# A DeltaNet and Fourier-mixing kernel on one core: two rounds of triangular inverses in turn, and the weights' conversion moved behind the first Fourier stage

## The chip, the cores and the metric

The kernel runs on one core of one Trainium2 chip. The metric is device microseconds (us) of one execution, smaller is better. Before the change the median of three runs is 840.67 us (838.32 to 844.29); the profiled execution took 837.88 us, of which the profile shows a span of 836.1 us.

The engines are TensorE (PE; its weight loads are shown as PEld), VectorE (DVE), ScalarE (ACT), GpSimd (POOL) and SyncE (SP), whose queue issues nearly all transfers here. Each engine works through its own instructions in order; semaphores order the engines among each other.

## The reference, cut to what matters

```python
# q, k, v: (4, 8, 768, 48) float32; beta: (4, 8, 768); w_ch1: (384, 1536), w_ch2: (1536, 384)
def _attn_ref(q, k, v, beta):                      # DeltaNet, token by token
    k_n = k / (norm(k) + 1e-06)
    for t in range(S):
        y[:, :, t] = q[:, :, t] @ state
        v_old = k_n[:, :, t] @ state
        state = state + beta[:, :, t] * outer(k_n[:, :, t], v[:, :, t] - v_old)
    return y

def _moe_ref(x, w_ch1, w_ch2):                     # x: y as (4, 768, 384)
    mixed = real(fft(fft(x, axis=1), axis=2))      # Fourier mixing
    u = x + mixed
    un = (u - mean(u)) / sqrt(var(u) + 1e-06)      # per row
    return u + maximum(un @ w_ch1, 0.0) @ w_ch2    # two-layer network
```

The two weight matrices reach the kernel as 64-bit floats. The kernel reads them as pairs of 32-bit integers and builds 32-bit floats from them with integer and float operations ("conversion").

## The kernel before

The tokens are worked on in groups of 128 (two chunks of 64), six groups to a batch of 768, 24 in all. Four groups make a round: the 32-by-32 triangular blocks of a round are inverted together, all 128 partitions side by side. The inverse is a loop of 31 steps, each of two VectorE operations, and every operation needs the result of the one ahead of it:

```python
def invert(r):                       # one round = 4 groups
    A = wk.tile([128, W, W], F32, tag="A", bufs=2); M = wk.tile([128, W, W], F32, tag="M")
    nc.gpsimd.memset(M, 0.0)
    nc.vector.transpose(A, G...)     # L291
    yield
    ...                              # norms of the keys: some 12 small VectorE operations, L298-314
    yield
    for j in range(W - 1):           # W = 32
        n = W - 1 - j
        t = wk.tile([128, 256], F32, tag="tmp")
        nc.vector.tensor_tensor(t, A[:, j+1:W, j:j+1]..., M[:, j:j+1, 0:j+1]..., op=ALU.mult)   # L320
        nc.vector.tensor_tensor(M[:, j+1:W, 0:j+1], M[:, j+1:W, 0:j+1], t, op=ALU.add)         # L323
        yield
    nc.vector.transpose(A..., M); nc.vector.transpose(G..., M...)                              # L326, L327
```

Around it stand, for each group g:

```python
def pre_a(g):   # keys: 4 transposes on PE -> KT (ACT L260), then 32 products K K^T (pair<-KT)
                # -> G (blocks to invert, ACT L279) and GX (the other blocks, ACT L281)
def pre_b(g):   # queries: 4 transposes -> QT (ACT); yield
                # K Q^T (pair<-QT,KT), masked into LQ (DVE L352); yield
                # mixing with the inverse: V scaled and MT built on GpSimd (L359, L363), two sets of
                #   32x32 products (one<-G,GX and one<-A,XM, evicted by ACT); yield; yield
                # W and U0 from MT, K and V (pair<-MT,K and one<-V,MT; ACT L403, L405)
def step(g, c): # the serial part, per chunk: S x W (PE) -> U (DVE L423) -> K x U (PE) -> S (DVE L442);
                # after the second chunk the output x: S x Q and U x LQ (PE), ACT L463, DVE L472
```

`fourier(b)` folds x into even and odd halves (GpSimd L489, L490; DVE L493 to L500), multiplies with two tables on PE (`pf`, `pb`) and adds the result to x with the statistics for the normalization (DVE L538 to L546). `mlp(b)` works on two tiles of 128 tokens at a time: transposes, 12 column blocks of the hidden layer (`ph`, evicted into `hT` by ACT L578 and DVE L580 in turn), then the second layer (`po`). 

The weights come in six pieces of 1536 elements per partition:

```python
def weights():
    n1, n2 = 1, DFF // DM            # w1 by blocks of 128 rows, w2 by four of them: 3 + 3 pieces
    ...
    w64s = [staged(0), staged(1)]    # staged: a tile of tag "big" (two buffers) and its transfer, L209
    yield
    for i, (_, dst) in enumerate(pieces):
        w64 = w64s[i]
        if 0 < i < len(pieces) - 1: w64s.append(staged(i + 1))
        lo, hi = w64[:, :, 0], w64[:, :, 1]
        man = wk.tile([128, DFF], F32, tag="F"); num = wk.tile([128, DFF], I32, tag="O")
        nc.scalar.activation(man, lo, Copy, ...)                      # L222
        nc.vector.tensor_scalar(num, hi, 0xFFFFF, ...)                # L223
        nc.vector.scalar_tensor_tensor(man, num, 2.0**-20, man, ...)  # L225
        yield
        num = wk.tile([128, DFF], I32, tag="O")
        nc.vector.tensor_scalar(num, hi, 20, 0x7FF, ...)              # L229
        nc.scalar.activation(num, num, Relu, bias=low_e)              # L231
        yield
        nc.vector.tensor_scalar(num, num, 255, 2.0**23, ...)          # L233
        nc.vector.scalar_tensor_tensor(num, hi, -2**31, num, ...)     # L235
        nc.gpsimd.tensor_tensor(dst, man, num, op=ALU.mult)           # L237
        yield
```

Tag "big" also holds the folded halves E of `fourier` and the hidden layer `hT` of `mlp`; tag "O" also holds O of `fourier`.

The driver: four `pre_a`, the queries of group 0, the inverse of round 0 alone, the rest of group 0; then twelve steps of batch 0, beside each of which run the preparation of the next group, the keys and the inverse of the next round, and half of the conversion. This part is in an order fixed by hand; from there on a list scheduler orders the program when it is built.

```python
with tc.manual_schedule(engines=engines):
    for g in range(RL): drain(pre_a(g)) ...
    pb = pre_b(0); drain(part(pb, 2)); drain(invert(0)); drain(pb)
    for n in range(2 * NL): one(n)          # steps of batch 0 and what goes beside them
for b in range(B):
    f = fourier(b)
    if b == 0: drain(f); drain(side)        # rest of the conversion
    else: run([(f, 1), (side, 1)])
    side, done = mlp(b), 0
    if b + 1 < B:
        for n in range(2*NL*(b+1), 2*NL*(b+2)): one(n)   # steps of batch b+1, with mlp(b) beside them
drain(side)
```

Of the kernel before, what the change touches and what calls it, by code (L numbers as in the profile page):

```python
# [58 lines left out]
def kernel(  # L59
# [84 lines left out]
    def load(g):  # L144
        if g < NLT:
            nc.sync.dma_start(out=Qs[g % 2][:, :, 0:D], in_=rows(q, g))
            halves(Ks[g % 3].rearrange("p (c j) d -> p c j d", c=2)[:, :, :, 0:D], k, g)
            Vs[g] = wk.tile([128, 2, 4, D], F32, tag="V", bufs=2, name="V")
            halves(Vs[g], v, g)
# [42 lines left out]
    def weights():  # L192

        if moe_w_ch1.dtype == F32:
            nc.sync.dma_start(out=w1, in_=moe_w_ch1.rearrange("(c p) f -> p c f", p=128))
            nc.sync.dma_start(out=w2, in_=moe_w_ch2.rearrange("(c p) m -> p c m", p=128))
            return
        w1v = moe_w_ch1.bitcast(I32).rearrange("(c p) (f two) -> p c f two", p=128, two=2)  # L200
        w2v = moe_w_ch2.bitcast(I32).rearrange("(c p) (m two) -> p c m two", p=128, two=2)
        n1, n2 = 1, DFF // DM
        pieces = [(w1v[:, i:i + n1], w1[:, i:i + n1]) for i in range(0, KD, n1)]
        pieces += [(w2v[:, i:i + n2], w2[:, i:i + n2]) for i in range(0, KF, n2)]

        def staged(i):
            t = wk.tile([128, DFF, 2], I32, tag="big", bufs=2, name="w64")
            src = pieces[i][0]
            nc.sync.dma_start(out=t.rearrange("p (c f) two -> p c f two", c=src.shape[1]), in_=src)  # L209
            return t  # L210

        w64s = [staged(0), staged(1)]
        yield
        for i, (_, dst) in enumerate(pieces):
            w64 = w64s[i]
            if 0 < i < len(pieces) - 1:
                w64s.append(staged(i + 1))
            lo, hi = w64[:, :, 0], w64[:, :, 1]
            man = wk.tile([128, DFF], F32, tag="F", name="man")
            num = wk.tile([128, DFF], I32, tag="O", name="num")  # L220

            nc.scalar.activation(man, lo.bitcast(U32), ACT.Copy, scale=2.0 ** -52, bias=1.0)  # L222
            tc.keep_in_program_order(nc.vector.tensor_scalar(num, hi, 0xFFFFF, None,  # L223
                                                             op0=ALU.bitwise_and))
            nc.vector.scalar_tensor_tensor(man, num, 2.0 ** -20, man, op0=ALU.mult, op1=ALU.add)  # L225
            yield

            num = wk.tile([128, DFF], I32, tag="O", name="num")
            tc.keep_in_program_order(nc.vector.tensor_scalar(  # L229
                num, hi, 20, 0x7FF, op0=ALU.logical_shift_right, op1=ALU.bitwise_and))  # L230
            nc.scalar.activation(num, num, ACT.Relu, bias=low_e)  # L231
            yield
            tc.keep_in_program_order(nc.vector.tensor_scalar(num, num, 255, 2.0 ** 23,  # L233
                                                             op0=ALU.min, op1=ALU.mult))
            nc.vector.scalar_tensor_tensor(num, hi, -2 ** 31, num, op0=ALU.bitwise_and,  # L235
                                           op1=ALU.bitwise_or)
            nc.gpsimd.tensor_tensor(dst.rearrange("p c f -> p (c f)"), man,  # L237
                                    num.bitcast(F32), op=ALU.mult)
            yield
# [11 lines left out]
    def pre_a(g):  # L251
# [13 lines left out]
        X = GXs[g] = wk.tile([128, 8, W], F32, tag="GX", bufs=6, name="GX")  # L265
# [19 lines left out]
    def invert(r):  # L285
# [3 lines left out]
        M = wk.tile([128, W, W], F32, tag="M", name="M")  # L289
# [3 lines left out]
        nrm = wk.tile([128, W], F32, tag="nrm", name="nrm")  # L293
        bn = wk.tile([128, W], F32, tag="bn", name="bn")
# [21 lines left out]
        for j in range(W - 1):  # L316
            n = W - 1 - j
            t = wk.tile([128, 256], F32, tag="tmp", name="tmp")
            t = t[:, 0:n * (j + 1)].rearrange("p (a b) -> p a b", a=n)
            nc.vector.tensor_tensor(t, A[:, j + 1:W, j:j + 1].broadcast_to([128, n, j + 1]),  # L320
                                    M[:, j:j + 1, 0:j + 1].broadcast_to([128, n, j + 1]),
                                    op=ALU.mult)
            nc.vector.tensor_tensor(M[:, j + 1:W, 0:j + 1], M[:, j + 1:W, 0:j + 1], t, op=ALU.add)  # L323
            yield
# [6 lines left out]
    def pre_b(g):  # L331

        r, li = divmod(g, RL)
        K, Q, KT, V = Ks[g % 3], Qs[g % 2], KTs.pop(g), Vs.pop(g)
        X = GXs.pop(g)
        QT = wk.tile([128, 2, 2, 128], F32, tag="QT", bufs=2, name="QT")
# [4 lines left out]
        nc.scalar.activation(QT.rearrange("p h j t -> p (h j t)"), pt, ACT.Copy)  # L341
        yield
        LQ = wk.tile([128, 2, 4, C], F32, tag="LQ", bufs=2, name="LQ")
# [12 lines left out]
        yield  # L356
        MTd, Md, nT = rounds[r]
# [15 lines left out]
        XM = wk.tile([128, 8, W], F32, tag="XM", bufs=2, name="XM")  # L373
# [32 lines left out]
        pre[g] = (K, QT, LQ, WT, U0)  # L406
# [72 lines left out]
    def fourier(b):  # L479
# [21 lines left out]
        yield  # L501
# [114 lines left out]
    side = weights()  # L616
# [3 lines left out]
    pb = inv = None  # L620

    def one(n):

        nonlocal pb, inv, side, done
# [5 lines left out]
        live = [(step(g, c), 1)]  # L630
        if g + 1 < NLT:
            if c == 0:
                load(g + 2)
                pb = pre_b(g + 1)
            if ri == 7 and not last_round:
                drain(inv)
            live.append((part(pb, 2 if ri == 6 else 3), 1))
        if not last_round:
            if ri < 4:
                if ri == 0:  # L640
                    load_beta(r + 1)
                live.append((pre_a(nxt + ri), 1))
                if ri == 3:
                    inv = invert(r + 1)
            elif ri < 7:
                live.append((part(inv, 12), 3))
        if b == 0:
            if i in (1, 7, 8, 9, 10, 11):
                live.append((part(side, 1 if i in (1, 11) else 2), 1))
        else:  # L650
            want = (PIECES - KEEP) * (i + 1) // (2 * NL)
            live.append((part(side, want - done), 2))
            done = want
        run(live)
# [3 lines left out]
    with tc.manual_schedule(engines=engines):  # L658
        for g in range(RL):
            drain(pre_a(g))  # L660
            if g < 2:
                load(g)
# [3 lines left out]
        pb = pre_b(0)  # L666
        drain(part(pb, 2))
        drain(invert(0))
        drain(pb)
        for n in range(2 * NL):  # L670
            one(n)
    for b in range(B):
        f = fourier(b)
        if b == 0:
            drain(f)
            drain(side)
        else:
            run([(f, 1), (side, 1)])
        side, done = mlp(b), 0
        if b + 1 < B:  # L680
            for n in range(2 * NL * (b + 1), 2 * NL * (b + 2)):
                one(n)
# [31 lines left out]
```

## Time and profile before

| engine | busy us | share of the span | instructions |
|---|---|---|---|
| PE (matmuls) | 697.1 | 83% | 10344 |
| PEld (weight loads) | 538.5 | 64% | 10344 |
| DVE | 416.2 | 50% | 980 |
| ACT | 197.5 | 24% | 452 |
| POOL | 111.7 | 13% | 122 |

The span is 836.1 us. The page cuts it into 40 slices of 20.9 us and gives the busy share of each engine in tenths, and PEclk, the clock granted to TensorE, in tenths of full speed. In the list of transfers the weights are six of 1536 KB; keys, queries and values come in 192 KB tiles (keys and values for the steps as four transfers of 48 KB). Times in a timeline are counted from the start of the span; a line gives start, length, engine, source line, operation, output and inputs, and how many instructions are merged in it.

### The profile page before, as it was taken

The page shows a single profiled execution, that of the slowest core. Times are in us where ns is not written, and L with a number is a line of the kernel's source. Part 1 is how long each engine was busy: PE and PEld are TensorE (multiplying, and loading weights), DVE is VectorE, ACT ScalarE, POOL GpSimd, SP SyncE. Part 2 cuts the span into 40 slices and gives each one's busy share as a digit, 9 for nine tenths or more (in the row PEclk, how much of TensorE's full clock was granted, in tenths as well). Part 3 has the DMA queues.
Part 4 walks back from the last instruction along what each step waited for, and adds up shares of the span by engine and source line. Part 5 has one row for each costly group of instructions (what it writes and reads, how often), then busy time and mean ns, then how long its engine had stood idle before and what let it go on. Part 6 is the DMA issues. An engine that isn't in the chain of part 4 may idle for free.

```text
span 836.1 us, 23182 instructions
## 1 busy us (share of the span) xinstructions
PE 697.1 (83%) x10344; PEld 538.5 (64%) x10344; DVE 416.2 (50%) x980; ACT 197.5 (24%) x452; POOL 111.7 (13%) x122
## 2 busy tenths in 40 slices
PE   5039436669577999889999999899999999999998
PEld 3027335558455786677776766776868767776775
DVE  0951694767998127952427921599513123431110
ACT  3014203433230331222331222321212212110010
POOL 1012002440413000230000111200100020000000
PEclk9999655557569899999999999999999999999999
DMA  6434212512210222200221111100211000000000
GB/s 111 119 139 82 41 30 72 163 33 90 65 40 15 45 50 40 49 16 9 45 51 40 40 35 42 24 7 27 38 35 31 3 20 1 10 10 19 10 11 19
DMA packets 109206, 36.06 MB, mean 43 GB/s; under 512 B 103633, under 2 KB 106930, under 8 KB 108722
## 3 DMA queue, kind: packets, MB, share of 16 engines
q1 hardware_dynamic: 107922, 34.28, 17.8%
q8 instruction: 81, 1.33, 0.7%
q10 hardware_dynamic: 1184, 0.30, 0.3%
q14 instruction: 19, 0.16, 0.1%
HBM read 29.84 MB, written 4.72 MB: 41 GB/s over the span
## 4 chain that ended last, share of the span: by engine, by line
PE 58%; DVE 28%; issue 4%; ACT 3%; POOL 2%; SPq 2%; DMA 1%; DVEq 0%; ACTq 0%; POOLq 0%
PE ph L104 18%; PE po L104 17%; PE pair L104 9%; DVE tmp L320 7%; DVE M L323 7%; PE one L104 5%; PE pf L104 3%; PE pb L104 3%; PE one L107 3%; SPq L136 1%; DVE A L326 1%; DVE G L327 1%; DVE A L291 1%; DVE O L493 1%; POOL w L237 1%
## 5 line engine op out<-in xcount | busy, mean ns | idle before, releaser
L104 PE MATMUL ph<-unT,w 128*128 128x256 f32 x864 | 211.9, 398 | 9.7 <-ACT unT L569 3.0
L104 PE MATMUL po<-w,hT 128*128 128x384 f32 x576 | 196.5, 491 | 3.1 <-DVE hT L580 2.4
L104 PEld LDWEIGHTS ph<-unT,w 128*128 128x128 f32 x864 | 164.7, 197 | 36.8 <-DVE hT L580 4.8
L104 PEld LDWEIGHTS po<-w,hT 128*128 128x128 f32 x576 | 106.6, 190 | 68.4 <-issue 2.7
L580 DVE TENSOR_SCALAR hT<-ph 128x256 f32<-128x256 f32 x72 | 30.3, 421 | 114.4 <-PE ph L104 114.3
L320 DVE TENSOR_TENSOR tmp<-A,M 128x31 f32<-128x31 f32 (+15 forms) x186 | 70.3, 378 | 5.0
L323 DVE TENSOR_TENSOR M<-M,tmp 128x31 f32<-128x31 f32 (+15 forms) x186 | 68.0, 365 | 5.1
L578 ACT ACTIVATE hT<-ph 128x256 f32<-128x256 f32 x72 | 27.6, 383 | 127.1 <-PE ph L104 122.1
L104 PE MATMUL one<-G,GX 32*32 32x32 f32 x768 | 19.1, 204 | 45.4 <-DVE G L327 45.2
L590 DVE TENSOR_TENSOR x<-x,po 128x384 f32<-128x384 f32 x24 | 13.2, 550 | 76.1 <-PE po L104 76.1
L104 PEld LDWEIGHTS one<-G,GX 32*32 32x32 f32 x768 | 16.2, 118 | 51.6 <-issue 40.0
L104 PE MATMUL one<-V,MT 64*64 64x48 f32 x768 | 47.6, 243 | 0.5 <-ACT MT L387 0.5
L363 POOL TENSOR_TENSOR MT<-A,pack 128x512 f32<-128x512 f32 x24 | 24.9, 1041 | 173.1 <-PE one L104 97.5
L104 PE MATMUL pair<-MT,K 64*64 64x64 f32 x768 | 44.4, 260 | 3.7 <-issue 3.0
L359 POOL TENSOR_TENSOR V<-V,nT 128x384 f32<-128x384 f32 x24 | 20.5, 853 | 183.1 <-DVE nrm L309 51.3
L104 PEld LDWEIGHTS one<-V,MT 64*64 64x64 f32 x768 | 44.3, 162 | 0.9 <-ACT MT L387 0.6
L104 PEld LDWEIGHTS pair<-MT,K 64*64 64x64 f32 x768 | 40.8, 154 | 4.7 <-issue 4.1
L376 ACT ACTIVATE XM<-one 32x256 f32<-32x256 f32 x48 | 18.0, 375 | 107.6 <-PE one L104 106.8
L104 PEld LDWEIGHTS pair<-U,K 64*64 64x64 f32 x704 | 16.9, 150 | 33.1 <-DVE U L423 16.6
L442 DVE TENSOR_TENSOR S<-S,pair 128x192 f32<-128x192 f32 x40 | 14.0, 351 | 47.1 <-PE pair L104 47.1
L104 PE MATMUL pair<-U,K 64*64 64x48 f32 x704 | 23.3, 245 | 16.2 <-DVE U L423 15.1
L104 PE MATMUL pair<-KT 48*32 48x64 f32 x1536 | 23.1, 249 | 11.8 <-DVE S L442 8.6
(99 smaller groups left out, 902.6 us busy)
## 6 DMA issues: line engine op xcount, KB each, us to landing
w<-in_moe_w_ch_dram SPq DMA_DIRECT2D x6, 1536.0 KB
Q<-in_q_dram SPq DMA_DIRECT2D x24, 192.0 KB
K<-in_k_dram SPq DMA_DIRECT2D x96, 48.0 KB
V<-in_v_dram SPq DMA_DIRECT2D x96, 48.0 KB
out_dram<-x SPq DMA_DIRECT2D x24, 192.0 KB
C<-in_k_dram SPq DMA_DIRECT2D x23, 192.0 KB
evt<-k_even SPq DMA_DIRECT2D x1, 579.0 KB
odt<-k_odd SPq DMA_DIRECT2D x1, 576.0 KB
```

Of the source, the lines that this page charges most:

```text
L104: nc.tensor.matmul(o, lhsT=lhsT, rhs=rhs, start=start, stop=stop, skip_group_check=True)
L107: nc.tensor.matmul(o, lhsT=src, rhs=ident[0:src.shape[0], 0:src.shape[0]], is_transpose=True, start=start, stop=True, skip_group_check=True)
L136: nc.sync.dma_start(out=dst[hh * C:hh * C + C, c], in_=src[b, 4 * hh:4 * hh + 4, t0:t0 + C, :].rearrange("j t d -> t j d"))
L320: nc.vector.tensor_tensor(t, A[:, j + 1:W, j:j + 1].broadcast_to([128, n, j + 1]), M[:, j:j + 1, 0:j + 1].broadcast_to([128, n, j + 1]), o ...
L323: nc.vector.tensor_tensor(M[:, j + 1:W, 0:j + 1], M[:, j + 1:W, 0:j + 1], t, op=ALU.add)
L359: nc.gpsimd.tensor_tensor(V.rearrange("p c j d -> p (c j) d"), V.rearrange("p c j d -> p (c j) d"), nT[:, m8, None].broadcast_to([128, 8, ...
L363: nc.gpsimd.tensor_tensor(MT, MTd[:, m8, None, :].broadcast_to([128, 8, 2, W]), m_blk[:, None, :, None].broadcast_to([128, 8, 2, W]), op=A ...
L376: nc.scalar.activation(XM[rw].rearrange("p m s -> p (m s)"), px[rw, 0:8 * W], ACT.Copy, scale=-1.0)
L442: nc.vector.tensor_tensor(s1v, s0.rearrange("p h j e -> p h (j e)"), pk, op=ALU.add)
L578: nc.scalar.activation(hT[:, fc, :], ph, ACT.Relu)
L580: nc.vector.tensor_scalar(hT[:, fc, :], ph, 0.0, None, op0=ALU.max)
L590: nc.vector.tensor_tensor(x[:, T, :], x[:, T, :], po, op=ALU.add)
```

## The change

Three things are reordered; the arithmetic stays as it was.

- **Two inverses in turn.** The keys of all eight groups of rounds 0 and 1 are prepared at the start. The inverse of round 0 starts alone; from step 13 on the inverse of round 1 runs in turn with it, a step of the one and a step of the other. `M`, `tmp`, `nrm` and `bn` get a second buffer for that.
- **Queries of batch 0 beside the inverses.** `pre_b` is split into `pre_q` (queries) and `pre_m` (mixing). `pre_q` of all six groups of batch 0 runs while the inverses do, into two tiles that hold all six groups (QT6 in tag "F", LQ6 in tag "big").
- **Conversion behind the first Fourier stage.** Nothing of the weights is loaded or converted beside batch 0. After `fourier(0)`, beside which now the keys of round 2 are prepared, all pieces are converted, and `mlp(0)` comes after them. There are twelve pieces of 768 elements, `w1` cut by columns, and both temporaries of a piece are halves of one tile in tag "O".

```diff
-        n1, n2 = 1, DFF // DM
-        pieces = [(w1v[:, i:i + n1], w1[:, i:i + n1]) for i in range(0, KD, n1)]
+        n1, n2 = DFF // (2 * KD), DFF // (2 * DM)
+        pieces = [(w1v[:, :, i:i + n1], w1[:, :, i:i + n1]) for i in range(0, DFF, n1)]
...
-            t = wk.tile([128, DFF, 2], I32, tag="big", bufs=2, name="w64")
+            t = wk.tile([128, DFF // 2, 2], I32, tag="big", bufs=2, name="w64")
...
-        w64s = [staged(0), staged(1)]
-        yield
+        w64 = None
         for i, (_, dst) in enumerate(pieces):
-            w64 = w64s[i]
-            if 0 < i < len(pieces) - 1:
-                w64s.append(staged(i + 1))
+            w64 = staged(i)
+            yield
             lo, hi = w64[:, :, 0], w64[:, :, 1]
-            man = wk.tile([128, DFF], F32, tag="F", name="man")
-            num = wk.tile([128, DFF], I32, tag="O", name="num")
+            tmp = wk.tile([128, 2, DFF // 2], F32, tag="O", name="wtmp")
+            man, num = tmp[:, 0], tmp[:, 1].bitcast(I32)
...
-        X = GXs[g] = wk.tile([128, 8, W], F32, tag="GX", bufs=6, name="GX")
+        X = GXs[g] = wk.tile([128, 8, W], F32, tag="GX", bufs=8, name="GX")
...
-        M = wk.tile([128, W, W], F32, tag="M", name="M")
+        M = wk.tile([128, W, W], F32, tag="x" if r == 1 else "M", bufs=2 if r == 1 else 1,
+                    name="M")
...
-            t = wk.tile([128, 256], F32, tag="tmp", name="tmp")
+            t = wk.tile([128, 256], F32, tag="tmp", bufs=2, name="tmp")
...
-    def pre_b(g):
+    def pre_q(g, QT=None, LQ=None):     # transposes of the queries, K Q^T, mask
+    def pre_m(g):                       # mixing with the inverse, W, U0
...
         for g in range(RL):
-            drain(pre_a(g))
-            if g < 2:
-                load(g)
+            if g + 1 < RL:
+                advance(keys[g + 1])
+            drain(keys[g])
+        load_q(0)
+        load_q(1)
+        load_kv(0)
+        load_beta(1)
+        load_kv(1)
+        inv0, inv1 = invert(0), invert(1)
+        qs = [pre_q(g, QT6[:, g], LQ6[:, g]) for g in range(NL)]
+        advance(inv0, 2)
+        ...                             # keys 4 to 7 and queries 0, 1 beside steps 0 to 11 of inv0
-        pb = pre_b(0)
-        drain(part(pb, 2))
-        drain(invert(0))
-        drain(pb)
+        advance(inv1)
+        advance(inv0)
+        advance(inv1)
+        for g in range(2, NL):
+            drain(qs[g])
+            for _ in range(3):
+                advance(inv0)
+                advance(inv1)
+        while advance(inv0):
+            advance(inv1)
+        pm = pre_m(0)
+        while advance(pm):
+            advance(inv1, 2)
+        f = fourier(0)
         for n in range(2 * NL):
-            one(n)
+            ...                         # step, pre_m of the next group, 3 steps of inv1 (to step 5),
+            ...                         # the first two folds of fourier(0) at steps 8 and 10
+        keys = [pre_a(g) for g in range(2 * RL, 3 * RL)]
+        advance(f)
+        for k4 in keys:
+            advance(k4)
+            advance(f)
+            advance(k4)
+        drain(f)
+        inv = invert(2)
+    side = weights()
+    drain(side)
     for b in range(B):
-        f = fourier(b)
-        if b == 0:
-            drain(f)
-            drain(side)
-        else:
-            run([(f, 1), (side, 1)])
+        if b > 0:
+            run([(fourier(b), 1), (side, 1)])
         side, done = mlp(b), 0
```

## The prediction

> **What bounds the kernel now.** I read the slices of the page first. The rows are PE, DVE and the granted PE clock:
>
> ```profile
> PE   5039436669577999889999999899999999999998
> DVE  0951694767998127952427921599513123431110
> PEclk9999655557569899999999999999999999999999
> ```
>
> PE is nearly full from slice 13 on. Before that it is idle in slice 1, where DVE is full, and often half idle until 270 us at a low clock. The busy time by stretches (PE, PEld, DVE, ACT, POOL, each with its instructions, then PE clock, DMA share, GB/s) puts numbers to it:
>
> ```profile
> 0.00:54.00 54.00, 11.15 (x310) 8.34 (x311) 31.79 (x80) 8.44 (x16) 5.07 (x19) 1.00 0.57 141
> 54.00:216.00 162.00, 108.57 (x2646) 94.86 (x2646) 99.73 (x213) 53.52 (x113) 33.49 (x30) 0.69 0.30 69
> 216.00:267.00 51.00, 35.43 (x288) 26.41 (x288) 50.09 (x85) 11.93 (x15) 14.70 (x5) 0.75 0.13 38
> 267.00:836.00 569.00, 541.92 (x7104) 408.85 (x7102) 234.62 (x604) 123.61 (x309) 58.44 (x69) 0.98 0.12 27
> ```
>
> So there are four parts: the first inverse alone (to 54), batch 0 and its Fourier stage (to 216), a stretch with DVE full (50.09 of 51 us: third inverse and the last three pieces of conversion), and 569 us bound by PE. The chain that ended last shows the steady rate at the end:
>
> ```profile
> 768.23 15.81 PE ph L104 x72
> 784.04 15.49 PE po L104 x48
> 801.29 15.81 PE ph L104 x72
> ```
>
> That is 0.220 us per ph matmul and 0.323 us per po matmul. With these, and for the small matmuls the merged timeline of 76 to 91 us (16 of S x W in 0.45, 64 of the keys' products in 0.85), I weigh the PE order of both kernels: 642 us in all. At 267 us the kernel before has 111 of them behind it, and takes 569 us for the other 531, 38 us of loss. **The time is therefore: when PE becomes full, plus what PE has left then, plus some 35 us.**
>
> Next, DVE in the inverse beside a step (timeline):
>
> ```profile
> 108.78 0.42 DVE L323 TENSOR_TENSOR M<-M,tmp 128x255 f32<-128x255 f32 x1
> 109.24 0.42 DVE L320 TENSOR_TENSOR tmp<-A,M 128x256 f32<-128x256 f32 x1
> 109.69 0.43 DVE L323 TENSOR_TENSOR M<-M,tmp 128x256 f32<-128x256 f32 x1
> 110.04 0.55 DVE L472 TENSOR_TENSOR x<-x,pair 128x384 f32<-128x384 f32 x1
> ```
>
> A dependent operation starts 0.03 to 0.04 us after the end of the last one (109.24 to 109.69: 0.45 for 0.42), an independent one 0.08 before its end (110.04). Taking turns wins 0.12 us wherever the neighbour is independent. Last, the conversion, on DVE and on POOL:
>
> ```profile
> 217.09 0.93 DVE L223 TENSOR_SCALAR num<-w 128x1536 int32<-128x1536 int32 x1
> ...
> 226.36 3.47 DVE L320 TENSOR_TENSOR tmp<-A,M 128x240 f32<-128x240 f32 x1
> ...
> 230.51 0.94 DVE L223 TENSOR_SCALAR num<-w 128x1536 int32<-128x1536 int32 x1
> ```
>
> ```profile
> 225.96 3.61 POOL L237 TENSOR_TENSOR w<-man,num 128x1536 f32<-128x1536 f32 x1 [4.81 <-DVE num L235]
> ```
>
> A piece takes 13.4 us from one L223 to the next. While POOL multiplies, a DVE operation that elsewhere takes 0.41 us takes 3.47.
>
> **What the Trainium skill says.** (1) "SBUF — State Buffer", section Who interferes with whom: a DVE instruction with two SBUF inputs is blocked by a GpSimd instruction that reads SBUF, for the whole of it. The trace agrees: 3.47 us at 226.36 ends with POOL's 3.61. (2) "VectorE: DVE Perf Modes", section The DRAIN you can't avoid: the next operation waits until the pipe is empty, but one that is not held starts earlier. The trace agrees in the sense used here: 0.45 against 0.35 us. (3) "TensorE: Matmul & The Clock Gate", section What's actually happening: idleness throttles the PE clock to half. The trace agrees in kind: four key transposes take 1.10 us at 4.52 and 0.66 at 82.38. The row PEclk says 1.0 at 4 us all the same, so I go by durations. The page lets the clock rise after some 3.4 us of activity; here PE worked from 54 on and was slow until 76.
>
> **The change, part by part.** Times are ends on the new time axis.
>
> *Two inverses, to 73 us (54 before).* The four key groups are pipelined: 1.1 us of transposes and 1.1 of products each in place of a period of 2.9, so the first G is ready at 14.1. The prelude takes 26.71 - 19.77 = 6.9 us, one mask of queries 0.6: 21.6. Twelve steps alone (26.71 to 35.23 before) 8.5 and a mask 0.6: 30.7. Now DVE's order has the transpose of round 1. Its last key tile stands on SP behind K, V, eight beta transfers, K and V of groups 0 and 1; at 2.7, 3.1 and 5.5 us as in the trace SP comes to it at 30, so with transfer, transposes, products I put that G at 36. A wait of 5 us. Prelude again, 7.5: 43.5. Then 18 steps of either round in turn: 13.97 + 14.0 as they were alone, four masks 2.4, less 36 changes of round x 0.12 = 4.3: 69.6. Two transposes 3.6: **73**.
>
> *Batch 0, to 141 (pf starts at 184 before).* First mixing and first step 8.7 (53.99 to 62.69 before), second step 8: 90. A group holds 5.3 us of PE at full clock, with its DVE hand-overs 7.5, at half clock 10.4. I take 9 for four groups, 126; the two early folds on DVE cost 4, the last group without mixing 6: 136. One fold is left (GpSimd 2, DVE 2.5): 141. Gone: the second inverse from between the steps, half the conversion, and the 3.5 us multiplications.
>
> *Fourier, to 160 (pb starts at 199.6 before).* pf and four key groups are 13.6 us of PE at full clock, 23 at half; I take 19. The lead is now 40 us.
>
> *Conversion, to 258.* DVE comes to the first piece behind the pb additions: 17.5 us in the trace, I take 16.5: 176.5. All twelve pieces now stand here, in place of six of that size. A piece goes around ACT, DVE, ACT, DVE, POOL on one buffer: by half of the durations of 1536 plus 0.06 each, 0.85 + 0.87 + 0.46 + 0.85 + 0.46 + 0.87 + 1.8 and six hand-overs of 0.1 = 6.8 us. With the third inverse between its operations 7.6 for some 8.3 pieces, 7.0 for 2.7: 82. Only after eleven pieces is a buffer of tag "big" free for hT, so PE, after two column blocks, has only the steps of batch 1 until **258.5**.
>
> *PE, to the end.* In the new order 103 us of matmuls stand ahead of that point (30 ph and 12 po fewer than at 267 before, 1.5 groups of steps more), so 539 are left. 258.5 + 539 + 35 = 832.5. A measured time is 1.8 above the span of the page (837.88 against 836.1): **834 us**. The 40 us won up to pb are nearly all paid back by 29 us more of conversion in a stretch where DVE is full, and 8 us of matmuls that PE has not done yet.
>
> **Rivals.** (a) *The lead stays.* If the conversion hid behind the steps of batch 1, up to 40 us would come through: about 797. For it: PE has those steps to do. Against: hT has no buffer before piece eleven, and steps share DVE with conversion. (b) *DVE is fuller than the loop.* Its operations between first piece and eleventh sum to 34 (pieces) + 22 (inverse) + 7 (steps) = 63, and eleven POOL multiplications block it for up to 16.5: 79.5. If this and the loop don't overlap as I assume, or ACT waits in order for evictions of a slow PE, T is 10 to 15 us later: 845 to 850. (c) *The clock rises early.* With a full clock in batch 0 and Fourier (7 + 6 us) and no wait for the key tile (5 us): 816.
>
> **Range and chances.** (b) and (c) are the ends of what I can't settle, (a) is unlikely at full size: 816 to 850. 2% faster is below 823.9; that needs (c) or a part of (a): 0.24. 2% slower is above 857.5, beyond (b): 0.06. Within 2%: 0.70.
>
> **What would show it.** In the changed profile: first transposes of M for round 0 at about 73 us, with a DVE wait near 31; pf from about 141; the first weight operation on DVE at about 176; pieces 7 to 7.6 us apart with DVE full; ph in long rows from about 258; then PE as full as before. It is wrong if long rows of ph come before 245 (conversion hidden) or after 275, or if the last part takes a time much other than 574 us.

## The result and the profile after

The changed kernel takes 863.57 us (median of four runs, 862.90 to 865.07), the kernel before 840.7 beside it: a ratio of 1.0271 with a 95% interval of 1.0231 to 1.0310. It is 2.7% slower; predicted were 834 us and a range of 816 to 850. The profiled execution has a span of 861.3 us.

The slices of the changed kernel, the same three rows as before (PE, DVE, granted PE clock), now of 21.5 us each:

```profile
PE   5323876985008999899999989889999999999998
DVE  3598423467995225970626831489512232331110
PEclk9555565855555999899999999999999999979999
```

Three things differ. The clock row reads mostly 5 from slice 1 to slice 12 (21 to 280 us), where before it read 9 up to slice 3 and 5 to 7 from slice 4 to slice 11. The first slices are no real difference: in the kernel before, four transposes of the queries take 1.11 us at 62.19, against 0.66 us for four of the keys at 82.38, so PE was slow there too although the row says 9. PE stands at 0 for two slices (215 to 258 us) under a DVE at 9. And there is a 7 near the end (slice 35, from 754 us) that the kernel before doesn't have. The busy time by stretches, cut at the events that the prediction named (columns as before):

```profile
0.00:76.00 76.00, 27.20 (x760) 21.03 (x760) 50.08 (x136) 16.38 (x34) 5.73 (x19) 0.65 0.46 83
76.00:186.00 110.00, 89.07 (x2160) 80.08 (x2160) 48.72 (x129) 34.97 (x88) 21.77 (x26) 0.64 0.25 52
186.00:278.00 92.00, 35.88 (x807) 30.17 (x806) 74.84 (x142) 29.35 (x45) 28.46 (x21) 0.54 0.38 105
278.00:861.00 583.00, 556.11 (x6618) 418.85 (x6618) 235.52 (x606) 119.91 (x298) 55.97 (x65) 0.97 0.11 25
```

The third line is the late conversion: 92 us in which PE works for 36. In batch 0 and the Fourier stage (second line) PE is busy for 89 of 110 us at a mean clock of 0.64, and DVE, no longer converting, for 49. After 278 it takes 583 us. The chain at the end has one row longer than the other of its kind:

```profile
758.37 18.00 PE ph L104 x72
...
793.62 15.81 PE ph L104 x72
809.43 15.49 PE po L104 x48
```

The first inverse's two transposes of M start at 72.42 and 74.17 and end at 76.1; the mixing's first products (pf) stand at 144.89, pb at 162.52. DVE in between did what was foreseen except for one wait; timeline of DVE, with the idle time ahead of an operation and what ended it in brackets:

```profile
30.61 0.41 DVE L326 TENSOR_TENSOR M<-M,tmp 128x240 f32<-128x240 f32 x1
39.07 1.92 DVE L294 STREAM_TRANSPOSE A<-G 128x1024 f32<-128x1024 f32 x1 [8.05 <-ACT G L281]
```

The wait for the last key tile of round 1 is 8.05 us, not 5: PE starts the tile's transposes, once its transfer has landed, only at 35.54.

### The profile page after: what moved, and what is told of

It is laid out like the page before. It is cut to its first block, busy times and chain, and to the rows that moved or that the text cites. A ratio compares the mean times of both kernels' runs of the same rounds, so it can differ in the third digit from the quotient of the medians.

```text
span 861.3 us, 23214 instructions
## 1 busy us (share of the span) xinstructions
PE 708.3 (82%) x10344; PEld 550.1 (64%) x10344; DVE 409.2 (48%) x1010; ACT 200.6 (23%) x464; POOL 111.9 (13%) x128
## 4 chain that ended last, share of the span: by engine, by line
PE 60%; DVE 26%; POOL 4%; ACT 3%; issue 3%; SPq 3%; DMA 2%; ACTq 0%; DVEq 0%; POOLq 0%
PE ph L104 20%; PE po L104 16%; PE pair L104 10%; PE one L104 6%; DVE M L326 5%; DVE tmp L323 5%; PE pf L104 3%; PE one L107 2%; SPq L136 2%; PE pb L104 2%; POOL w L238 2%; DVE G L330 1%; DVE A L294 1%; PE ptr L107 1%; DVE A L329 1%
## 5 line engine op out<-in xcount | busy, mean ns | idle before, releaser
L104 PEld LDWEIGHTS ph<-unT,w 128*128 128x128 f32 x864 | 167.7, 200 | 38.6 <-DVE hT L591 6.7
L104 PE MATMUL one<-G,GX 32*32 32x32 f32 x768 | 19.5, 207 | 66.8 <-DVE G L330 66.8
L323 DVE TENSOR_TENSOR tmp<-A,M 128x255 f32<-128x255 f32 (+15 forms) x186 | 70.2, 378 | 3.8
L326 DVE TENSOR_TENSOR M<-M,tmp 128x255 f32<-128x255 f32 (+15 forms) x186 | 68.5, 368 | 5.2
L104 PE MATMUL one<-V,MT 64*64 64x48 f32 x768 | 50.6, 250 | 0.7 <-ACT MT L398 0.5
L104 PE MATMUL pair<-MT,K 64*64 64x64 f32 x768 | 48.5, 272 | 2.1 <-ACT MT L398 1.6
L104 PEld LDWEIGHTS pair<-MT,K 64*64 64x64 f32 x768 | 43.3, 163 | 3.6 <-ACT MT L398 2.0
L104 PE MATMUL pair<-S,WT 48*64 48x48 f32 x704 | 23.7, 249 | 15.8 <-DVE S L453 13.5
L104 PEld LDWEIGHTS pair<-S,WT 48*64 48x64 f32 x704 | 17.7, 155 | 25.2 <-DVE S L453 14.9
L398 ACT ACTIVATE MT<-one 32x256 f32<-32x256 f32 x48 | 17.9, 373 | 62.8 <-PE one L104 60.6
L107 PE MATMUL one<-pack,C 128*128 128x128 f32 x96 | 19.4, 339 | 15.7 <-DMA C<-in_k_dram 15.6
```

Of the source, the lines that this page charges most:

```text
L104: nc.tensor.matmul(o, lhsT=lhsT, rhs=rhs, start=start, stop=stop, skip_group_check=True)
L107: nc.tensor.matmul(o, lhsT=src, rhs=ident[0:src.shape[0], 0:src.shape[0]], is_transpose=True, start=start, stop=True, skip_group_check=True)
L398: nc.scalar.activation(MT[rw, :, 1, :], py[rw, 0:8 * W].rearrange("p (m s) -> p m s", s=W), ACT.Copy)
```

## The experiments

Each ratio is to the kernel before, run on the same chip beside it. Ratios leave out executions more than 1.5% above the fastest of their kernel, so they needn't be the quotient of two medians. Where a kernel leaves part of the work out, it is said.

### Without the conversion (a_noconv, b_noconv)

Both kernels with the weights set to a constant instead of loaded and converted; what is left is the order of everything else.

```diff
+    nc.gpsimd.memset(w1, 0.02)
+    nc.gpsimd.memset(w2, 0.02)
     def weights():
+        return
```

> The kernel before with the same left out. Its last three pieces (40 us of DVE, in part beside the third inverse) and the first three beside batch 0 go. Theory P: 805 to 815, so that without conversion the kernel after is the faster of the two, by 5 to 15 us. Theory C: the kernel before stays some 20 us the faster one.

Measured: 798.86 us, ratio 0.9534 (0.9488 to 0.9580).

> The kernel after, with the loading and the conversion of the weights left out (both weight tiles filled with a constant at the start). Theory P (place): the loss is the twelve pieces in a stretch where DVE is full and PE has nothing to run; without them only the third inverse (some 30 us) stands there, so the 90 us of conversion shrink to 30 and the time falls by about 60, to 795 to 808. Theory C (clock): PE's half clock between 80 and 150 us and after 165 makes the loss; the time falls by no more than 25, to about 840.

Measured: 806.68 us, ratio 0.9636 (0.9597 to 0.9675). That number lies within theory P's range, the other doesn't, and the order of the two kernels is the wrong way round. My theory fell here: I held that the front part, two inverses in turn, was a gain which the late conversion ate. The changed order is 1.0% slower when nobody converts. So a second cause had to be found, one that has nothing to do with the weights.

### Conversion elsewhere: a_six, b_late, a_stageF, a_inv2first

a_six puts the six pieces of 1536 of the kernel before into the changed kernel, still late. b_late is the kernel before with its early half of the conversion moved behind the Fourier stage and nothing else changed:

```diff
-            if i in (1, 7, 8, 9, 10, 11):
-                live.append((part(side, 1 if i in (1, 11) else 2), 1))
```

> The kernel after with the six pieces of 1536 of the kernel before (two temporaries in tags F and O), still all behind the Fourier stage. Rival S: the whole loss is in the halved pieces, so 835 to 842. Theory P: twelve halves took 90 us, 7.6 each in the middle; six wholes at 13.4 take 80: at most 10 us less, 852 to 862.

Measured: 858.19 us, ratio 1.0249 (1.0198 to 1.0300), where the changed kernel has 1.0271. The size of the pieces is not it.

> The kernel before with one part of the change alone: no conversion beside batch 0, all six pieces behind the Fourier stage. Theory P: batch 0 gets shorter by 10 to 15 us (its stalls behind the multiplications and the 1.5 MB transfers go), the stretch behind longer by three pieces of 13.4 = 40: 862 to 872. Rival: the conversion beside batch 0 costs as much there as behind (some 40 us), so that 838 to 845 stays.

Measured: 848.92 us, ratio 1.0088 (1.0054 to 1.0121): a miss for both numbers. The late place alone costs 0.9%, much less than I had put on it.

Both stage their late pieces in tag "big", and in both PE stands still for some 23 us, at different places. PE timelines of b_late and then of a_six:

```profile
255.43 1.06 PE L104 MATMUL one<-G,GX 32*32 32x32 f32 x32 [22.84 <-DVE G L327]
```

```profile
254.37 4.96 PE L104 MATMUL ph<-unT,w 128*128 128x256 f32 x12 [22.63 <-ACT hT L590]
```

The first waits 22.84 us for the third inverse, the second 22.63 for a first eviction into `hT`. In the changed kernel ACT's timeline shows what such an eviction waits for: the last read of a piece's raw weights (L235, of piece eleven), which frees the staging tile in "big".

```profile
277.58 0.38 ACT L589 ACTIVATE hT<-ph 128x256 f32<-128x256 f32 x1 [1.16 <-DVE wtmp L235]
```

a_stageF takes that second wait away: the changed kernel with its pieces staged as two halves of one tile of tag "F", which is free by then, so that `hT` finds its buffer in "big".

```diff
-            t = wk.tile([128, DFF // 2, 2], I32, tag="big", bufs=2, name="w64")
+            if i == 0:
+                wf.append(wk.tile([128, 2, DFF // 2, 2], I32, tag="F", name="w64"))
+            t = wf[0][:, i % 2]
```

> The kernel after, with the raw weights staged in the tile of tag F (free after the Fourier stage) and not in tag big, so that the hidden layer has its buffer at once. Theory P: ph can follow each converted block, 16 to 25 us of PE work fall into the 44 us in which PE waits, T comes that much earlier: 838 to 850. Rival S (sizes of the pieces: twelve of 768 cost more than six of 1536): nothing changes, 860 to 868.

Measured: 849.44 us, ratio 1.0137 (1.0094 to 1.0180), 1.3% below the changed kernel. In the changed kernel PE does one row of twelve ph at 197.33 and the next at 278; here the rows follow each other as their pieces of w1 come, and the releaser is the conversion itself:

```profile
197.06 4.16 PE L104 MATMUL ph<-unT,w 128*128 128x256 f32 x12 [3.16 <-POOL w L242]
206.18 5.49 PE L104 MATMUL ph<-unT,w 128*128 128x256 f32 x12 [3.15 <-POOL w L242]
```

In the stretch from 186 to 278 PE works 61 us instead of 36:

```profile
186.00:278.00 92.00, 61.10 (x635) 41.21 (x633) 72.37 (x136) 28.54 (x44) 27.84 (x17) 0.75 0.35 100
```

a_inv2first goes the other way: it finishes the third inverse ahead of the conversion.

```diff
         inv = invert(2)
+        drain(inv)
```

> The kernel after with the third inverse finished ahead of the conversion (same operations, another order on DVE). PE waits 44 us there for this inverse. Theory P in the form that the buffer of the hidden layer is what holds PE: steps of batch 1 run earlier, but ph starts no earlier (inverse 30, then twelve pieces at 6.8 = 82, from 187: 299), 865 to 880. If the inverse is what holds PE: 845 or less.

Measured: 875.33 us, ratio 1.0439 (1.0373 to 1.0506). PE then gets its 32x32 products earlier, at 223.73 instead of 255.87, and the kernel is longer: its long rows of ph come at 313.91, after 19.44 us of idle time that an eviction into `hT` ended. The steps are not the limit of this stretch, the buffer of `hT` is.

### The loop on VectorE: a_dvemul

The last multiplication of a piece on DVE instead of POOL.

```diff
-            nc.gpsimd.tensor_tensor(dst, man.rearr..., op=ALU.mult)
+            nc.vector.tensor_tensor(dst, man.rearr..., op=ALU.mult)
```

> The changed kernel with the last multiplication of each piece on VectorE instead of GpSimd. Prediction's step 4 had a loop of 6.8 to 7.6 us a piece, of which GpSimd's 1.85 us block VectorE; on VectorE the multiplication of 768 elements should take about 0.95 as the other operations of two inputs do. Theory L (the loop's length is VectorE's work and what blocks it): twelve pieces shorter by 0.9 us each, 851 to 857. Rival T (the transfer or the space sets the pace): 860 to 865.

Measured: 852.96 us, ratio 1.0191 (1.0147 to 1.0234); theory L. In the changed kernel (DVE and POOL timelines) two pieces start 7.65 us apart, POOL multiplies for 1.96, and a DVE operation that takes 0.41 us elsewhere is held for 1.95:

```profile
215.23 0.55 DVE L224 TENSOR_SCALAR wtmp<-w 128x768 int32<-128x768 int32 x1
...
221.00 1.95 DVE L323 TENSOR_TENSOR tmp<-A,M 128x252 f32<-128x252 f32 x1
222.88 0.55 DVE L224 TENSOR_SCALAR wtmp<-w 128x768 int32<-128x768 int32 x1
```

```profile
220.71 1.96 POOL L238 TENSOR_TENSOR w<-wtmp 128x768 f32<-128x768 f32 x1 [5.66 <-DVE wtmp L235]
```

In a_dvemul the product takes 0.95 us and comes every 6.92:

```profile
213.05 0.95 DVE L238 TENSOR_TENSOR w<-wtmp 128x768 f32<-128x768 f32 x1
...
219.97 0.95 DVE L238 TENSOR_TENSOR w<-wtmp 128x768 f32<-128x768 f32 x1
```

So in its middle the loop did run as the prediction worked it out. And giving DVE more work made the kernel faster, since DVE was blocked for longer (1.95 us) than it now works (0.95). This is what the Trainium skill says in "SBUF — State Buffer", section Who interferes with whom (the port pair that both engines share is an exclusive lock), with a size for this case: 0.73 us a piece.

### Half of the conversion early: a_early, a_earlyF, a_best

a_early converts six pieces beside the steps of batch 0, one staging buffer, and leaves all folds behind the last step. a_earlyF adds a_stageF's staging for the other six.

> The kernel after with six of the twelve pieces (all of the first layer) converted beside the steps of batch 0, and the folds of the Fourier stage after the last step. Theory P: batch 0 gets longer by about 12 us (six pieces put some 2 us each into the order of DVE), the stretch behind shorter by six pieces of 7.6 = 45: 825 to 838. Theory C: the lower clock stays, so no more than 10 us better, 853 or above.

Measured: 857.95 us, ratio 1.0205 (1.0153 to 1.0258): a miss for theory P. The number is theory C's, but the trace shows another cause than the clock.

> As the last, and the six pieces of the second layer staged in tag F, so that nothing keeps the hidden layer from its buffer: ph may start behind the Fourier stage, at about 195. Theory P: another 15 to 25 us of PE work move into the stretch that DVE fills: 805 to 822, faster than both kernels. If only DVE's fill counts and not the buffer: as the last run.

Measured: 848.66 us, ratio 1.0071 (1.0026 to 1.0117): a miss too. DVE's timeline in a_early shows waits that the theory lacked; with `LQ6` in the other buffer of "big" a piece can't be loaded while the last one is converted:

```profile
114.82 0.56 DVE L224 TENSOR_SCALAR wtmp<-w 128x768 int32<-128x768 int32 x1 [4.57 <-DMA w<-in_moe_w_ch_dram]
...
129.23 0.56 DVE L224 TENSOR_SCALAR wtmp<-w 128x768 int32<-128x768 int32 x1 [4.16 <-DMA w<-in_moe_w_ch_dram]
```

Steps wait behind this DVE: the last x comes at 163.1 instead of 144.2. a_best mends it: two halves of one "big" tile, loaded two ahead, pieces only beside steps 0 to 7, folds at steps 8 and 10 as in the changed kernel, the last four pieces in "F".

```diff
-            w64 = staged(i)
-            yield
+            w64 = w64s[i]                       # two loaded ahead
...
+            if n < 8:
+                live.append((part(side, 3 if c else 2 if n else 0), 1))
```

> Six of the twelve conversion pieces beside the steps of batch 0, but staged two ahead in two slots, so that no piece waits for its transfer, and the folds of the x tiles stay at their steps. The other six pieces stay behind the Fourier stage, two staged before it and four in the space of F, so that hT's space is free. Theory P (VectorE is idle two thirds of the time between 86 and 150 us, so a piece whose data are there costs little beside the steps; what the single staging slot cost before was the wait of 3.5 to 4.6 us for each transfer): last x at 145 to 152 us, late conversion about 45 us instead of 90, whole kernel 815 to 832. Rival R (VectorE runs in order, so each piece delays the step's own operations by its 3.5 us whether its data are there or not): last x after 160, kernel 842 to 858.

Measured: 840.14 us, 824.69 to 850.41, ratio 0.9894 (0.9855 to 0.9933); the median is neither number. The spread is wide and the ratio rests on four of twelve executions, the lowest; the median of all twelve is 0.3% above the 837.67 of the kernel before. That a_best is faster than the kernel before is not shown.

### The front part: a_keys2_noconv, then the pause

The kernel before makes the keys of round 2 beside batch 0, the changed kernel in the Fourier stage. a_keys2_noconv is a_noconv with these keys beside steps 6 to 9 and the third inverse begun at step 10; a_best2 is a_best with the same.

> The changed kernel without loading and conversion of the weights (constants instead), and with the keys of round 2 made beside steps 6 to 9 of batch 0 and the third inverse begun at step 10. Theory K (the front part loses its lead because round 2's keys and inverse come only after the Fourier stage, while VectorE is idle beside the late steps of batch 0): 788 to 799, that is 8 to 18 below the 806.7 of the changed kernel without conversion, and at or below the 798.9 of the kernel before without conversion. Rival H (TensorE at half clock is what batch 0 waits for, so the moved products only make it longer by what they save later): 803 to 810.

Measured: 811.06 us, ratio 0.9675 (0.9640 to 0.9710), no better than a_noconv, and 1 us above rival H's range. Theory K fell.

> Both together, with conversion: six pieces beside steps 0 to 7, keys of round 2 beside steps 6 to 9, third inverse from step 10, six pieces behind the Fourier stage in the space of F. Theory P with K: 806 to 822, faster than both kernels. With P but not K: 815 to 832. With R: 840 to 858.

Measured: 838.44 us, ratio 0.9993 (0.9969 to 1.0017); neither number.

What the traces without conversion did show is a gap of PE among the last products of the Fourier stages of later batches, and a halved clock after it (1.24 us up to 537.41 in a_noconv, then 0.50 from 540 to 550). The diff that I read has a line for it which I had passed over; the diff above leaves it out as well. In `fourier`, the pause after the folds has moved into the loop over three tiles:

```diff
             nc.vector.tensor_tensor(o[:, :, 1:ND], o[:, :, 1:ND], back, op=ALU.add)
-        yield
+            yield
```

For batch 0 this serves the early folds. For batches 1 to 3, `fourier(b)` runs by turns with the last nine pieces of `mlp(b-1)`, one for each pause. Three pauses in place of one use up two pieces before there is mixing to fill. PE timeline of the kernel before, ahead of the last batch:

```profile
728.09 2.77 PE L104 MATMUL po<-w,hT 128*128 128x384 f32 x8
730.70 1.94 PE L104 MATMUL pb<-dtab,F 97*128 97x97 f32 x16
732.95 0.52 PE L107 MATMUL ptr<-pack,un 128*128 128x128 f32 x3 [0.30 <-DVE x L539]
```

and of the changed kernel:

```profile
746.24 2.77 PE L104 MATMUL po<-w,hT 128*128 128x384 f32 x8
748.85 1.03 PE L104 MATMUL pb<-dtab,F 97*128 97x97 f32 x8
750.95 2.42 PE L104 MATMUL pb<-dtab,F 97*128 97x97 f32 x16 [1.07 <-DVE x L601]
753.67 1.99 PE L104 MATMUL pb<-dtab,F 97*128 97x97 f32 x8 [0.30 <-DVE x L550]
```

Before, five rows of eight po products stand between the pb products behind the last pf; after, three (from 739.32 on). The po products run out two tiles early, PE waits 1.07 us for DVE, and eight pb take 1.99 us instead of 1.03.

The pause put back for batches 1 to 3:

```diff
+            if b == 0:
+                yield
+        if b > 0:
             yield
```

> The changed kernel without loading and conversion of the weights, with the pause of fourier after its folds put back to one for the later batches (the change made it one per tile, three, so the perceptron's last nine pieces are used up two pauses earlier). Theory Y (TensorE then has a gap of 1 to 3 us ahead of the mixing of the third and of the last batch, after which its clock is half for 5 to 17 us; the traces show 13.6 us of lost clock there without conversion, and 1.7 us in the kernel before): 795 to 801, the 8 us that the changed kernel without conversion is behind the kernel before without it. Rival H (the loss is in the packed steps of batch 0, which TensorE does at half clock): 804 to 809.

Measured: 797.46 us, ratio 0.9492 (0.9435 to 0.9549). Theory Y: it is 1.4% below a_noconv, and level with b_noconv.

> The changed kernel whole, with that one pause alone put back for the later batches. Theory Y: 852 to 859, that is 5 to 11 below the changed kernel. Rival H: 861 to 866.

Measured: 855.49 us, ratio 1.0173 (1.0100 to 1.0245). Theory Y again, 1.0% below the changed kernel, the half-widths of the two ratios being 0.40% and 0.73%. The busy time by stretches before the last batch, in the changed kernel and in a_yield:

```profile
752.00:756.00 4.00, 3.70 (x20) 3.39 (x19) 3.73 (x14) 0.66 (x2) 0.82 (x2) 0.58 0.08 32
756.00:760.00 4.00, 2.84 (x9) 1.86 (x8) 2.93 (x9) 1.21 (x3) 0.11 (x1) 0.50 0.00 2
760.00:764.00 4.00, 4.00 (x14) 3.24 (x13) 0.51 (x2) 0.38 (x1) 0.93 (x2) 0.64 0.00 0
```

```profile
752.00:756.00 4.00, 2.54 (x13) 1.74 (x12) 3.76 (x13) 1.21 (x3) 0.00 (x0) 0.83 0.13 49
756.00:760.00 4.00, 4.00 (x16) 3.32 (x15) 0.73 (x3) 0.38 (x1) 0.92 (x2) 0.74 0.00 0
```

The clock column (third from the end) is under 0.65 for three stretches, against 0.83 and 0.74 for two. The kernel before, at the same point of its last batch:

```profile
732.00:736.00 4.00, 2.53 (x16) 1.85 (x16) 3.58 (x13) 1.35 (x4) 0.00 (x0) 1.00 0.13 49
```

PE is idle here for as long as in a_yield (2.53 and 2.54 of 4 us busy) and keeps its full clock. So it is shown that the moved pause costs time; that it does so by the one gap and the clock behind it is not.

> The version with six pieces staged two ahead beside batch 0 and six behind the Fourier stage in the space of F, with the pause put back. Theory Y: 818 to 830, faster than the kernel before by 1 to 2.5%. Rival H: 826 to 842, as without it.

Measured: 831.59 us, ratio 0.9887 (0.9861 to 0.9913), in rival H's range and not in theory Y's. By the ratios (a_best has 0.9894) the pause brings nothing here, by the medians of all executions 1.2% (0.9912 of the kernel before against 1.0030); a_best is too spread to tell.

> The same with the keys of round 2 and the start of the third inverse beside batch 0, and the pause put back. Theory Y: 822 to 832. Rival H: 834 to 841, as without it.

Measured: 828.16 us, 827.64 to 830.06, ratio 0.9862 (0.9810 to 0.9914). Theory Y, 1.3% below a_best2. This is the fastest version, 1.4% below the kernel before and 4.0% below the changed one (0.9862 / 1.0271 = 0.960); a_best_y is not to be told from it. From 186 to 278 us PE works 77 us in it, where the changed kernel had 36:

```profile
186.00:278.00 92.00, 76.55 (x904) 57.60 (x905) 61.74 (x140) 28.81 (x59) 19.80 (x18) 0.83 0.19 53
```

### The half clock of batch 0: a_warm_noconv, a_warm

Products of 128x128 that nobody reads, put after the two state products of every step of batch 0: two of 386 columns in a_warm_noconv (on a_yield_noconv), one of 256 in a_warm (on a_best2_y).

```diff
+            if b == 0:
+                for _ in range(2):
+                    mm(ps_post([128, 386], "warm")[:, 0:386], ident, evt[:, 0, 0:386], True)
```

> The changed kernel without conversion and with the pause put back (797.5), and with two idle 128x128 by 386 products, whose result nobody reads, after each of the two state products of every step of batch 0. In that stage TensorE is busy some 7 of 10 us at a clock of 0.5 to 0.7 (between 80 and 150 us). Theory C (the clock stays half because small products with gaps don't count as enough activity, and full products in the gaps keep it up): clock above 0.9 between 100 and 150 us, 775 to 795. Rival N (the clock of this stage doesn't follow such filling, or the filling costs what it brings): 798 to 815.

Measured: 810.41 us, ratio 0.9683 (0.9627 to 0.9739).

> The best version so far (828.2), with one such product of 256 columns in each of these places. Theory C: 812 to 826. Rival N: 828 to 840.

Measured: 838.78 us, ratio 1.0012 (0.9980 to 1.0044). In both cases rival N, by its second half: the clock does follow, in a_warm in part (0.78 from 92 to 140 us, against 0.55 in a_best2_y), the time doesn't. Stretches of a_yield_noconv, where PE is busy for over 9 of 10 us and not 7, then of a_warm_noconv:

```profile
100.00:110.00 10.00, 9.41 (x300) 8.78 (x295) 2.23 (x6) 3.36 (x9) 1.52 (x2) 0.67 0.24 46
110.00:120.00 10.00, 9.50 (x272) 8.94 (x271) 1.88 (x5) 2.97 (x7) 2.12 (x3) 0.50 0.26 47
```

```profile
100.00:110.00 10.00, 9.04 (x221) 6.07 (x221) 3.13 (x6) 2.11 (x5) 1.83 (x2) 1.00 0.17 31
110.00:120.00 10.00, 9.94 (x224) 6.43 (x222) 1.06 (x3) 2.03 (x6) 1.83 (x2) 1.00 0.18 35
```

At full clock PE gets through fewer instructions in the same 10 us (224 against 272), since the filling takes its own time: four such products in a row hold PE for 1.5 us (109.47 to 110.96), and 22 such rows are some 33 us of PE, an estimate. The kernel takes 13 us longer, so the clock gave back less than those 33.

## Why the prediction was wrong, point by point

The time was 29.6 us above 834. Two steps of the prediction failed: *Conversion, to 258.5*, by 19.5 us, and *PE, to the end, 574*, by 9.3. The steps ahead of them were 2 to 4 us late. Why the change lost and didn't win is another sum.

Taken by ratios, the 2.71% fall into three parts that sum to it by the way they are taken. **Conversion:** 1 - 0.9534 = 4.66% in the kernel before, 1.0173 - 0.9492 = 6.81% in the changed one with the pause put back; the difference of 2.15%, with a half-width of about 1.0, is 18 us of 839. **The pause:** 1.0271 - 1.0173 = 0.98%, 8 us, with a half-width of about 0.8 (1.44% without conversion, 1.31% from a_best2 to a_best2_y). **The front part:** 0.9492 - 0.9534 = -0.42%, with half-widths of 0.57 and 0.46 not to be told from nothing. This part also holds two pieces of the change that the list of three doesn't name and no run takes back: `XM` has one buffer instead of two, and beside the later steps queries and mixing run as `pre_q` and `pre_m`.

*Two inverses, to 73.* Measured 76.1. The turns won what was foreseen; the wait near 31 was 8.05 us instead of 5, which is the whole difference of 3.

*Batch 0, to 141; Fourier, to 160.* pf came at 144.89, pb at 162.52: 4 and 2.5 us late. Right in kind and nearly in size. But "the lead is now 40 us" was read wrongly. Without conversion the kernel before has its pb at 173.79, not 198.79. So 25 of the 36 us of lead are work left out for later, and 11 come from the order. These 11 are not kept either. The kernel before in b_noconv, and the changed one in a_yield_noconv, by stretches from 84 us:

```profile
84.00:170.00 86.00, 55.88 (x1620) 48.37 (x1616) 49.75 (x125) 21.83 (x53) 14.11 (x15) 0.66 0.25 45
170.00:230.00 60.00, 55.85 (x675) 43.69 (x674) 45.91 (x135) 14.45 (x38) 7.38 (x11) 0.86 0.10 19
```

```profile
84.00:170.00 86.00, 69.42 (x1791) 62.99 (x1787) 31.93 (x75) 26.20 (x67) 17.30 (x18) 0.63 0.22 42
170.00:230.00 60.00, 56.06 (x701) 41.71 (x700) 42.79 (x126) 12.01 (x30) 7.37 (x11) 0.80 0.12 25
```

With the 1102 and 900 PE instructions ahead of 84 us, both have issued the same number by 230: 3397 and 3392, of the same kinds but for 16 products of `pre_m` (8 each of pair<-MT,K and one<-V,MT) and 8 of po. The kernel before does the queries and the mixing of group 6 ahead of its pb (150 to 157 us), the changed one behind (166 to 171), so the first state of batch 1 is written at 177.5 in the one and 180.0 in the other. A lead must be counted in work done, not at one named event.

*Conversion, to 258.5.* This step failed by its sizes: the long rows of ph came at 278.01, beyond the 275 set as the bound. The 19.5 us are 2.5 from pb, 7.7 until the first piece (24.2 us behind pb instead of 16.5), and 9.3 for the pieces (91.3 instead of 82). For the 7.7, DVE's timeline:

```profile
173.74 0.56 DVE L556 BATCH_NORM_STATS2 bst<-x 128x6 f32<-128x384 f32 x1
179.54 0.36 DVE L451 COPY S<-pair 128x192 f32<-128x192 f32 x1 [5.24 <-PE pair L104]
```

DVE, in its fixed order, waits 5.24 us for a first step of batch 1, which PE reaches only through the mixing, full and at a clock of 0.50 from 174 to 180:

```profile
174.00:180.00 6.00, 6.00 (x95) 5.65 (x96) 0.76 (x4) 1.80 (x4) 0.00 (x0) 0.50 0.19 35
```

I had taken the 17.5 us of the kernel before, where no such step stood between. No run takes this wait away by itself, so its worth in the end is not measured. For the 9.3: the middle pieces are 7.2 to 8.0 us apart, nearly as foreseen, the first two 10.6 and 10.0, the last two 9.1 and 8.8; the loop was right (a_dvemul), its edges were not. What holds PE meanwhile are two things, first the third inverse on the crowded DVE, then, for its ph, `hT`; PE's timeline:

```profile
255.87 1.06 PE L104 MATMUL one<-G,GX 32*32 32x32 f32 x32 [44.25 <-DVE G L330]
...
278.01 14.90 PE L104 MATMUL ph<-unT,w 128*128 128x256 f32 x60 [1.37 <-ACT hT L589]
```

The mechanism, no buffer for `hT` before piece eleven, was right (ACT's line at 277.58 above): with the buffer free (a_stageF) 1.3% come back, with the third inverse early and the buffer not free (a_inv2first) none.

*PE, to the end, 574.* It took 583.3. The term that failed is "35 us of loss", taken over from the kernel before; with the 539 us of matmuls that the prediction left for this part it is 44. Of the 9 us more, 3 are the rounding of 38 to 35. The moved pause, which does not appear in the prediction, is a part of the rest, but how much is open. Put back, it brings 8 us of the whole by the ratios; in the trace of a_yield, whose execution of 859.32 us is the slowest of four, the last part is 857.2 - 276.47 = 580.7 us, 2.6 less:

```profile
276.47 14.90 PE L104 MATMUL ph<-unT,w 128*128 128x256 f32 x60 [1.32 <-ACT hT L592]
```

*Rivals.* (a) did not happen: PE stood still in the stretch where it was to hide the conversion. (b) was nearest, T later through a fuller DVE and a slow PE, but was put at 10 to 15 us where it was 19.5. (c) failed by direction: the clock stayed low longer (0.50 from 76 to 100 us, where it was 0.82 before, and 0.54 from 186 to 278).

What stays open: what spreads a_best's executions over 26 us, how the moved pause costs its 1.0 to 1.4%, and some 4 of the 9 us of the last part.

## What to carry to other kernels

Before a lead at some event is counted as a gain, ask which work was moved behind that event, and leave that work out of both kernels once: the two runs without conversion showed in one step that the new order brought no gain. A moved pause in a generator that fills another engine's gaps is a change to every later use of it; read such one-line moves as closely as the large ones. When work is moved into a stretch, look for the buffer it holds there, not only for the engine it fills.

## What the runs showed of the hardware

PE can be nearly without a gap in the profile and still be granted half its clock: 9.50 of 10 us busy at 0.50 (a_yield_noconv, 110 to 120) with products of 64x64, 48x64 and 32x32. In the changed kernel it was 6.00 of 6.00 us at 0.50 (174 to 180), there with 128x128 transposes and pb products between the small ones. The Trainium skill, "TensorE: Matmul & The Clock Gate", section What's actually happening, has the clock released by about 3.4 us of activity. The trace doesn't agree if activity means that PE has work in the profile; adding 128x128 products to the steps of batch 0 gave 1.00 (a_warm_noconv, 110 to 120). That fits a reading in which it counts how much of the array works, which is not shown: size and length of the products changed together, and 174 to 180 had large ones too.

The clock after a short gap was not the same everywhere: under 0.65 for some 12 us after one of 1.07 us in the changed kernel (752 to 764), but 1.00 in the kernel before, with PE busy for 2.53 of 4 us (732 to 736).
